# Two chunks share half-height rest products: rest weights split into a high and a low tile, first stage in a fixed order

## The chip, the cores and the metric

The kernel runs on one core of one Trainium2 chip. The metric is device time in microseconds (us) of one execution; lower is better. TensorE (PE) multiplies, with a sequencer that issues weight loads (PEld) and matmuls; VectorE (DVE), ScalarE (ACT) and GpSimd (POOL) work elementwise; SyncE (SP) issues most transfers.

## The reference

A causal depthwise convolution with 7 softmaxed taps per head, followed by two gated feed-forward layers on 8192 tokens (2 sequences of 4096) of 192 features, with 2048 hidden features.

```python
w = softmax(weight)                                  # 8 heads x 7 taps
out[b, s, h] = sum_k w[h, k] * x_pad[b, s + k, h]    # 24 features per head
x = out.reshape(8192, 192)

h = x @ w_in;  g = h * np.clip(h + 3.0, 0.0, 6.0) / 6.0;               y = g @ w_out     # layer 1
h = y @ w_in2; g = np.where(h > 0, h, np.exp(np.minimum(h, 0)) - 1.0); z = g @ w_out2    # layer 2
```

## The kernel before, in words

**Tiles.** Tokens are taken in 16 blocks of 512 (256 of each sequence), on the free axis; features lie on partitions. The hidden features of a layer are 16 chunks of 128. A "chunk" in this text is one (layer, block, chunk) triple; there are 512 of them, in the list `slots` (lines 526 to 533). Block 0 and block 1 of layer 0 are interleaved by twos, then come the other blocks in turn.

**Precision.** The operands of a product are each split into a high part and a low remainder, and a product is the sum high x high, high x low, low x high. 192 features are one full tile of 128 partitions ("main") and a rest of 64. Main of the block is in the tiles opA (high) and opB (low); the rest's high and low parts lie in opC and opD, a part in either half of the partitions. Weights: `h` and `l` for main (128 partitions), and one tile `r` for the rest, in which the high part lies in the lower 64 partitions and the low part in the upper for even chunks, and the other way round for odd chunks.

**First product** (`mm1`, line 461): into one PSUM bank `h` of 128 hidden features x 512 tokens; there are three such banks. At full height (`half` = ALL) it is five matmuls: h x opA, h x opB, l x opA, r x opC, r x opD. At half height the lower and the upper 64 partitions are done by separate matmuls, three and either one or two of the rest for each half: five and four.

**Gate** (`gate`, line 485; `first_done`, line 724): ACT makes u from h (one operation in layer 0, two in layer 1), DVE makes g from u and h, which frees the bank. `split` then makes gh (ACT) and gl (DVE) of the chunk before. `run_jobs` (line 569) spends a budget of other work after each chunk: decoding, splitting and loading of weights (`prepare`, line 654), convolution of later blocks, splitting of the second layer's input, sums; jobs have due chunks, and what is due is issued whatever the budget.

**Second product** (`mm2`, line 506): five matmuls per height from gh, gl and wo into two banks, four chunks after the first product (LAG = 4).

**Order.** The start (line 673) is written out by hand, up to block 0's operands. The first 36 chunks (line 764) run at full height, for each chunk a first product, its gate and jobs, then the second product of the chunk four before; within this stage a scheduler orders the instructions of each engine. From there to the end (line 765) the order is by hand again: two streams, one for the lower 64 partitions and one for the upper, alternate matmul by matmul, the upper one BEHIND = 8 matmuls later. In a bank the upper half may start only when the lower has left it (a tiny POOL memset, `relay`, line 479, passes that on). The convolution's taps of blocks 0 and 1 are tensor products (`taps_tensor`, line 280, 28 matmuls), those of the others run on DVE.

Of the kernel before, what the change touches and what calls it, by code (L numbers as in the profile page):

```python
# [8 lines left out]
F32 = mybir.dt.float32  # L9
# [19 lines left out]
NB = 512  # L29
# [25 lines left out]
def conv_moe_moe2(ctx: ExitStack, tc: tile.TileContext, x, weight, w_in1, w_out1, w_in2, w_out2, out):  # L55
# [95 lines left out]
    def split_w(item, f):  # L151

        kind, l, a, e = item
        if kind == "out":
            v = f[:, :(e - a) * D].rearrange("p (f e) -> p f e", f=e - a)
            w = wo[l][:, a:e]
            act.copy(w[:, :, 0:D], v)
            yield  # L160
            for c0, c1, to in ((0, P, 2 * P), (P, D, D)):
                vec.tensor_tensor(out=w[:, :, to:to + c1 - c0], in0=v[:, :, c0:c1],
                                  in1=w[:, :, c0:c1].bitcast(F32), op=ALU.subtract)
            yield
            return
        w = {k: v[:, a * P:e * P] for k, v in wi[l].items()}
        if kind == "in":
            f = f[:, :(e - a) * P]
            act.copy(w["h"], f)
            yield  # L170
            vec.tensor_tensor(out=w["l"], in0=f, in1=w["h"].bitcast(F32), op=ALU.subtract)
        else:
            f = f[:, :(e - a) // 2 * P].rearrange("p (f c) -> p f c", c=P)
            r = w["r"].rearrange("p (f two c) -> p two f c", two=2, c=P)
            for k, h in enumerate((LO, UP)):
                act.copy(r[h, k], f[h])
            yield
# [120 lines left out]

    def conv_r(b):
        a = yield from taps_vector(b, 1)  # L300
        lh, hl = opnd[0, b][2:]
        T0, T1 = slice(0, HB), slice(HB, NB)
        act.copy(hl[LO, T0], a[LO])
        act.copy(lh[UP, T1], a[UP])
        yield
        act.copy(lh[UP, T0], a[LO])
        act.copy(hl[LO, T1], a[UP])
        yield
        vec.tensor_tensor(out=lh[LO, T0], in0=a[LO], in1=hl[LO, T0].bitcast(F32), op=ALU.subtract)
        vec.tensor_tensor(out=hl[UP, T1], in0=a[UP], in1=lh[UP, T1].bitcast(F32), op=ALU.subtract)  # L310
        yield
        act.copy(hl[UP, T0], lh[LO, T0].bitcast(F32))
        act.copy(lh[LO, T1], hl[UP, T1].bitcast(F32))
        yield

    def conv(b):
        opnd[0, b] = ring()
        yield from alternate(conv_main(b, taps_tensor if b < TENSOR_TAPS else taps_vector), conv_r(b))

    CONV = 2 * K + 6  # L320

    def ring():


        A = op.tile([P, NB], F32R, name="opA", tag="opA")
        Bt = op.tile([P, NB], F32R, name="opB", tag="opB")
        lh = op.tile([P, NB], F32R, name="opC", tag="opC")
        hl = op.tile([P, NB], F32R, name="opD", tag="opD")
        return A, Bt, lh, hl

    def feed(b):
        load_squares(b)
# [106 lines left out]

    def split_y(b):  # L440
        y0, yr = ys.pop(b)
        A, Bt, lh, hl = opnd[1, b] = ring()
        act.copy(A, y0)
        yield
        h, other = (UP, LO) if b % 2 else (LO, UP)
        hi, lo = (lh, hl) if b % 2 else (hl, lh)
        act.copy(hi[h], yr[h])
        vec.tensor_tensor(out=Bt, in0=y0, in1=A.bitcast(F32), op=ALU.subtract)
        yield
        act.copy(lo[other], hi[h].bitcast(F32))  # L450
        vec.tensor_tensor(out=lo[h], in0=yr[h], in1=hi[h].bitcast(F32), op=ALU.subtract)
        yield
        act.copy(hi[other], lo[h].bitcast(F32))
        yield


# [4 lines left out]
    def mm1(s, half):  # L461


        l, b, f = slots[s]
        A, Bt, lh, hl = opnd[l, b]
        w = {k: v[half, f * P:(f + 1) * P] for k, v in wi[l].items()}
        if half is not UP:
            hs[s] = ps_h.tile([P, NB], F32, name="h", tag="h")
        h = hs[s]
        low, high = half is not UP, half is not LO  # L470
        todo = [(w["h"], A), (w["h"], Bt), (w["l"], A)]
        if half is ALL or low == (f % 2 == 0):
            todo += [(w["r"], lh), (w["r"], hl)]
        else:
            todo += [(w["r"], hl if low else lh)]
        for i, (k, m) in enumerate(todo):
            mm = nc.tensor.matmul(h, k, m[half], start=low and i == 0, stop=high and i == len(todo) - 1)  # L477
# [56 lines left out]
    NS = len(slots)  # L534
    at = {sl: i for i, sl in enumerate(slots)}
    jobs = []
    WORK = {"first": 3883, "conv": 8522, "split": 1664, ("sum", 0): 1304, ("sum", 1): 2488}

    def alternate(*gens):
        gens = list(gens)  # L540
# [21 lines left out]
    def load(item):  # L562

        kind, _, a, e = item
        n = (e - a) * {"out": D, "in": P, "r": R}[kind]
        lo = {"out": n + 160, "in": n + 80, "r": 2 * n + 160}[kind]
        return n // 2 + 80 + n + 80 + lo + (2 * n + 180) // 5

    def run_jobs(s):
# [103 lines left out]
    with tc.manual_schedule():  # L673
        tp, tr = load_taps(), transposes(0)
        make_identity(nc, ident)
        load_rows(0)
        next(tp)
        ahead(0)
        nc.gpsimd.memset(three, 3.0)
        next(tp)  # L680
        next(tr)
        next(tr)
        for k in range(K):
            vec.tensor_scalar(out=diag[k], in0=ident, scalar1=taps[:, 0, k:k + 1], scalar2=None, op0=ALU.mult)
        for _ in range(2):
            next(main)
        r = conv_r(0)
        while ready[0] < FIRST0:
            next(weights)
            next(r, None)  # L690
        drain(r)
        load_rows(1)
        drain(main)
# [51 lines left out]
    sums = {}  # L745
    BOTH = at[0, 2, 0]

    def stream(half, slots1, behind):

        for s in slots1:  # L750
            if s < NS:
                yield from mm1(s, half)
            ends = s >= behind and half is UP and slots[s - LAG][2] == NF - 1
            if s < NS and half is not LO and not ends:
                first_done(s)
            if s >= behind:
                yield from mm2(s - LAG, half)
                second_done(s - LAG, half)
            if s < NS and ends:
                first_done(s)  # L760
            if s == NS - 1 and half is not LO:
                split(s)

    drain(stream(ALL, range(BOTH + LAG), LAG))
    with tc.manual_schedule():
        ends = {}
        n = {LO: 0, UP: BEHIND}
        for half in (LO, UP):
            for s in range(BOTH + LAG, NS + LAG):
                first = 5 if (half is LO) == (slots[s % NS][2] % 2 == 0) else 4  # L770
                if s < NS:
                    assert half is LO or n[half] > ends[s]
                    n[half] += first
                    ends[s] = n[half]
                n[half] += 5
        lower, upper = (stream(half, range(BOTH + LAG, NS + LAG), LAG) for half in (LO, UP))
        for _ in range(BEHIND):
            next(lower)
        going = [lower, upper]
        while going:  # L780
            for g in list(going):
                if next(g, jobs) is jobs:
                    going.remove(g)
        run_jobs(NS + 9)


# [28 lines left out]
```

## Time and profile before

| | |
|---|---|
| median of 3 runs | 1174.16 us (1173.98 to 1175.13) |
| the profiled execution | 1174.62 us |
| its span, first to last instruction | 1172.9 us |
| PE / PEld / DVE / ACT busy | 99% / 89% / 78% / 79% |
| stage at full height | about 15.8 to 102.8 us |
| two half-height streams | 102.8 to about 1166.5 us |

A row of the timeline gives the start (us from the span's start), the duration, the engine, the line, the operation, the tiles written and read, shapes and how many instructions were merged, and in brackets the idle time of the engine before it and what ended it. "64*128" is the height and width of a matmul's weights: 64 partitions contracted, 128 columns. A matmul's end is modelled and includes the way through the array, so successive matmuls overlap; the distance of their starts is what a matmul takes. L49 is the line of a helper through which all DVE and ACT operations go.

### The profile page before, as it was taken

How to read it: one execution, taken by the hardware profiler on the slowest of the kernel's cores; microseconds unless marked ns; L12 is line 12 of the kernel's file. 1: busy time of each engine (PE TensorE's matmuls, PEld its weight loads, DVE VectorE, ACT ScalarE, POOL GpSimd, SP SyncE). 2: the span in 40 equal slices, each digit the busy share in tenths (PEclk: the TensorE clock that was granted, in tenths of full speed). 3: DMA queues.
4: the chain of work that ended last, by engine and by line, in shares of the span. 5: the costliest groups of instructions: out<-in, count | busy, mean ns of one | idle time of the engine just before them, and what ended most of it. 6: DMA issues, size and time to landing. Idle time of an engine off the chain costs nothing.

```text
span 1172.9 us, 25129 instructions
## 1 busy us (share of the span) xinstructions
PE 1163.0 (99%) x9504; PEld 1045.5 (89%) x9504; DVE 919.7 (78%) x1560; ACT 929.8 (79%) x1684; POOL 44.9 (4%) x490
## 2 busy tenths in 40 slices
PE   8999999999999999999999999999999999999998
PEld 6778999999998889988899888997889998878777
DVE  7997999988887878868787787877877666677765
ACT  6876777778869787786877869778686888888885
POOL 0000000000000000000000000000000000000000
PEclk9999999999999999999999999999999999999999
DMA  6422011110010100101001010100000000000001
GB/s 181 107 67 42 20 42 46 29 28 1 2 28 1 28 1 5 25 1 28 2 11 18 1 29 1 21 9 1 15 2 15 2 8 8 15 15 15 13 6 26
DMA packets 105370, 26.80 MB, mean 23 GB/s; under 512 B 96416, under 2 KB 104096, under 8 KB 105248
## 3 DMA queue, kind: packets, MB, share of 16 engines
q1 hardware_dynamic: 104960, 24.99, 10.2%
q8 instruction: 74, 1.21, 0.4%
q14 instruction: 48, 0.39, 0.1%
q10 hardware_dynamic: 288, 0.20, 0.1%
HBM read 18.87 MB, written 6.29 MB: 21 GB/s over the span
## 4 chain that ended last, share of the span: by engine, by line
PE 97%; DVE 1%; ACT 1%; issue 0%; ACTq 0%; DVEq 0%
PE p L521 49%; PE h L477 47%; DVE acc L49 0%; ACT u L49 0%; DVE xw L49 0%; DVE wi0r L49 0%; ACT gh L49 0%; ACT opC L49 0%; ACT xw L49 0%; DVE cw L49 0%; PE pso L427 0%; ACT L49 0%; DVE wo L49 0%; ACT opD L49 0%; PE psx L243 0%
## 5 line engine op out<-in xcount | busy, mean ns | idle before, releaser
L521 PE MATMUL p<-gh,wo 64*128 64x512 f32 (+1 forms) x2976 | 639.9, 393 | 0.2 <-ACT gh L49 0.2
L49 DVE SCALAR_TENSOR_TENSOR g<-u,h 128x512 f32<-128x512 f32 x512 | 350.6, 685 | 222.7 <-ACT u L49 219.5
L521 PE MATMUL p<-gl,wo 64*128 64x512 f32 (+1 forms) x1984 | 517.7, 391 | 0.0
L521 PEld LDWEIGHTS p<-gh,wo 64*128 64x128 f32 (+1 forms) x2976 | 461.6, 185 | 34.2 <-ACT gh L49 0.7
L49 DVE TENSOR_TENSOR gl<-g,gh 128x512 fp32r<-128x512 f32 x512 | 350.3, 684 | 2.2 <-ACT gh L49 1.7
L521 PEld LDWEIGHTS p<-gl,wo 64*128 64x128 f32 (+1 forms) x1984 | 313.3, 161 | 17.0 <-DVE gl L49 0.5
L49 ACT CAST gh<-g 128x512 fp32r<-128x512 f32 x512 | 311.1, 608 | 10.4 <-DVE g L49 10.2
L49 ACT ACTIVATE u<-h,three 128x512 f32<-128x512 f32 x256 | 176.1, 688 | 139.1 <-PE h L477 137.6
L477 PE MATMUL h<-opA,wi1h 64*128 64x512 f32 x512 | 200.0, 399 | 0.0
L477 PE MATMUL h<-opA,wi1l 64*128 64x512 f32 x512 | 199.3, 398 | 0.0
L477 PE MATMUL h<-opB,wi1h 64*128 64x512 f32 x512 | 195.7, 390 | 0.0
L49 ACT ACTIVATE u<-h 128x512 f32<-128x512 f32 x256 | 152.6, 596 | 51.8 <-PE h L477 50.6
L477 PE MATMUL h<-opA,wi0h 64*128 64x512 f32 (+1 forms) x476 | 182.1, 396 | 0.5 <-DVE g L49 0.5
L477 PE MATMUL h<-opA,wi0l 64*128 64x512 f32 (+1 forms) x476 | 181.8, 395 | 0.0
L477 PE MATMUL h<-opB,wi0h 64*128 64x512 f32 (+1 forms) x476 | 180.5, 391 | 0.0
L49 ACT ACTIVATE u<-u 128x512 f32<-128x512 f32 x256 | 161.9, 632 | 8.1
L477 PE MATMUL h<-opD,wi1r 64*128 64x512 f32 x384 | 148.7, 393 | 0.0
L477 PE MATMUL h<-opC,wi1r 64*128 64x512 f32 x384 | 147.8, 390 | 0.0
L477 PE MATMUL h<-opD,wi0r 64*128 64x512 f32 (+1 forms) x366 | 141.0, 393 | 0.0
L477 PE MATMUL h<-opC,wi0r 64*128 64x512 f32 (+1 forms) x366 | 140.3, 391 | 0.6 <-ACT opC L49 0.6
L477 PEld LDWEIGHTS h<-opA,wi1h 64*128 64x128 f32 x512 | 94.2, 184 | 14.0 <-DVE g L49 5.2
L49 DVE SCALAR_TENSOR_TENSOR acc<-xT,taps,acc 128x256 f32<-128x256 f32 (+1 forms) x180 | 106.0, 601 | 0.1
(90 smaller groups left out, 1217.8 us busy)
## 6 DMA issues: line engine op xcount, KB each, us to landing
raw<-in_moe_w_out_dram SPq DMA_DIRECT2D x16, 384.0 KB, 3.3
out_dram<-z SPq DMA_DIRECT2D x180, 32.0 KB, 1.6
raw<-in_moe_w_in_dram SPq DMA_DIRECT2D x7, 512.0 KB, 4.5
x_sq<-in_x_dram SPq DMA_DIRECT2D x112, 32.0 KB, 2.2
raw<-in_moe_w_in_dram SPq DMA_DIRECT2D x8, 256.0 KB, 4.0
xr_sq<-in_x_dram SPq DMA_DIRECT2D x56, 32.0 KB, 2.1
x_sb<-in_x_dram SPq DMA_DIRECT2D x4, 128.0 KB, 3.7
raw<-in_moe_w_in_dram SPq DMA_DIRECT2D x4, 128.0 KB, 3.6
```

The costliest lines, as they stand in the source:

```text
L49: return fn(*args, **kw)
L477: mm = nc.tensor.matmul(h, k, m[half], start=low and i == 0, stop=high and i == len(todo) - 1)
L521: nc.tensor.matmul(p[:n], k[:, :n], m[half], start=first and not end and k is not w0l, stop=last and end == 1)
```

## The change

The tile `r` becomes two tiles of half the width, `r` (high) and `s` (low); in each, even chunks lie in the lower 64 partitions and odd chunks in the upper. opC and opD now hold the rest's high and low part in both halves alike. So the three rest products of a chunk (r x opC, r x opD, s x opC) are all half-height ones, for an even chunk in the lower half and for an odd one in the upper.

In the first 36 chunks two chunks are multiplied together (`mm1_pair`): six full-height matmuls, alternately for the one and the other chunk, and then six half-height ones, alternately lower half (even chunk) and upper half (odd chunk), into two banks. Then both gates with their jobs, then the second products of the two chunks four before, at full height as before. In the later stage the half of a chunk that holds its rest does six first-product matmuls, the other half three; the order of the first three is h x opA, l x opA, h x opB; BEHIND is 9.

The whole kernel now is in a fixed order. In the start, block 1's rows are loaded before block 0's taps; its convolution is written out (tensor taps behind the first pair, the rest's taps around the first gates) instead of being a job; weights are prepared up to FIRST = 4 instead of 5 pieces before the first pair. Splitting a piece of rest weights is one copy and one subtraction on 128 partitions instead of two each on 64.

```diff
-BEHIND = 8
+BEHIND = 9
-FIRST0 = 1
-FIRST = 5
-TENSOR_TAPS = 2
+FIRST = 4
...
-    wi = [{n: const.tile([P, FF], F32R, name=f"wi{l}{n}") for n in ("h", "l", "r")} for l in range(2)]
+    wi = [{n: const.tile([P, FF // (1 + (n in "rs"))], F32R, name=f"wi{l}{n}") for n in "hlrs"} for l in range(2)]
...
-            for k, h in enumerate((LO, UP)):
-                act.copy(r[h, k], f[h])
-            yield
-            for k, h, o in ((0, LO, UP), (1, UP, LO)):
-                vec.tensor_tensor(out=r[o, k], in0=f[h], in1=r[h, k].bitcast(F32), op=ALU.subtract)
+        pre = kind == "r"
+        hi, lo = (wi[l][k][:, (a >> pre) * P:(e >> pre) * P] for k in ("rs" if pre else "hl"))
+        f = f[:, :(e - a >> pre) * P]
+        act.copy(hi, f)
+        yield
+        vec.tensor_tensor(out=lo, in0=f, in1=hi.bitcast(F32), op=ALU.subtract)
...
-        todo = [(w["h"], A), (w["h"], Bt), (w["l"], A)]
-        if half is ALL or low == (f % 2 == 0):
-            todo += [(w["r"], lh), (w["r"], hl)]
-        else:
-            todo += [(w["r"], hl if low else lh)]
+        todo = w[0] + w[1] * ((half is LO) == (f % 2 == 0))
...
+    def first_parts(l, b, f, half):
+
+        A, Bt, C, Dt = opnd[l, b]
+        main = slice(f * P, (f + 1) * P)
+        rest = slice(f // 2 * P, (f // 2 + 1) * P)
+        return [(wi[l][k][half, main], m[half]) for k, m in (("h", A), ("l", A), ("h", Bt))], \
+               [(wi[l][k][half, rest], m[half]) for k, m in (("r", C), ("r", Dt), ("s", C))]
+
+    def mm1_pair(s):
+
+        pair = (s, s + 1)
+        parts = []
+        for t, half in zip(pair, (LO, UP)):
+            assert slots[t][2] % 2 == (half is UP)
+            hs[t] = ps_h.tile([P, NB], F32, name="h", tag="h")
+            parts.append(first_parts(*slots[t], ALL)[0] + first_parts(*slots[t], half)[1])
+        for i in range(6):
+            for t, todo in zip(pair, parts):
+                nc.tensor.matmul(hs[t], *todo[i], start=i == 0, stop=i == 5)
...
+    r, tr = conv_r(0), transposes(1)
+    next(main)
+    next(main)
+    for _ in range(K):
+        next(weights)
+        next(r)
+    for g in (r, r, weights, main, r, tr, r, tr, main):
+        next(g)
     while ready[0] < FIRST:
         next(weights)
-    drain(transposes(1))
...
-    job(conv(1), CONV, 0, at[0, 1, 0], WORK["first"])
...
-    drain(stream(ALL, range(BOTH + LAG), LAG))
...
+    opnd[0, 1] = ring()
+    main, r = conv_main(1, taps_tensor), conv_r(1)
+    mm1_pair(0)
+    next(main)
+    next(main)
+    for _ in range(3):
+        next(r)
+    for t in range(2):
+        raw_g[t] = gate(0, hs.pop(t))
+        split(t - 1)
+        next(r)
+        next(r)
+    for g in (r, r, main):
+        next(g)
+    drain(r)
+    drain(main)
+    for s in range(2, BOTH + LAG, 2):
+        mm1_pair(s)
+        for t in (s, s + 1):
+            first_done(t)
+        if s >= LAG:
+            for t in (s, s + 1):
+                drain(second(t - LAG, ALL))
```

## Rows read from the trace of the kernel before

**Rows 1.** The page, busy time: busy us, share of the span, instructions.
```profile
PE 1163.0 (99%) x9504; PEld 1045.5 (89%) x9504; DVE 919.7 (78%) x1560; ACT 929.8 (79%) x1684; POOL 44.9 (4%) x490
```
**Rows 2.** The page, chain that ended last, by engine.
```profile
PE 97%; DVE 1%; ACT 1%; issue 0%; ACTq 0%; DVEq 0%
```
**Rows 3.** The chain of waits in order of time: start, us, engine, tile, matmuls.
```profile
31.38 1.20 PE h L477 x4
...
33.04 1.17 PE h L477 x5
...
101.69 1.16 PE p L521 x5
...
160.59 0.93 PE h L477 x8
```
**Rows 4.** Windows: stretch, its length, busy us of each engine (instructions), clock, DMA.
```profile
31.38:102.69 71.31, 71.31 (x306) 55.96 (x306) 67.12 (x125) 55.79 (x101) 0.00 (x0) 1.00 0.29 74
```
**Rows 5.** Timeline near the end, PE and weight loads after a common standstill.
```profile
1162.57 0.19 PEld L521 LDWEIGHTS p<-gh,wo 64*128 64x128 f32 x2 [0.67 <-ACT gh L49]
1162.58 0.50 PE L521 MATMUL p<-gh,wo 64*128 64x512 f32 x2 [0.24 <-ACT gh L49]
```
**Rows 6.** Timeline where the stage at full height ends.
```profile
102.23 0.63 PE L521 MATMUL p<-gl,wo 128*128 128x512 f32 x2
102.23 0.19 PEld L521 LDWEIGHTS p<-gl,wo 128*128 128x128 f32 x1
...
102.78 0.18 PEld L477 LDWEIGHTS h<-opA,wi0h 64*128 64x128 f32 x1 [0.36 <-issue]
...
103.12 0.39 PE L477 MATMUL h<-opB,wi0h 64*128 64x512 f32 x1
```
**Rows 7.** Timeline in the start: from 8 rows to 128.
```profile
4.31 0.57 PE L207 MATMUL pt<-etap,heads 8*128 8x7 f32 x2
...
4.81 0.18 PEld L243 LDWEIGHTS psx<-ident,x_sb 128*128 128x128 f32 x1
```
**Rows 8.** Timeline of PE in the front: first matmul and waits.
```profile
15.76 0.96 PE L477 MATMUL h<-opA,wi0h 128*128 128x512 f32 x3
16.55 0.43 PE L477 MATMUL h<-opB,wi0h 128*128 128x512 f32 x1
...
27.23 0.50 PE L477 MATMUL h<-opA,wi0h 128*128 128x512 f32 x1 [0.47 <-DVE g L49]
...
31.38 0.50 PE L477 MATMUL h<-opC,wi0r 128*128 128x512 f32 x1 [0.63 <-ACT opC L49]
```
**Rows 9.** Timeline: last matmul of a chunk, its u and its g.
```profile
101.29 0.40 PE L477 MATMUL h<-opD,wi0r 128*128 128x512 f32 x1
...
101.79 0.69 ACT L49 ACTIVATE u<-h,three 128x512 f32<-128x512 f32 x1 [0.26 <-PE h L477]
...
102.51 0.69 DVE L49 SCALAR_TENSOR_TENSOR g<-u,h 128x512 f32<-128x512 f32 x1 [0.26 <-ACT u L49]
```
**Rows 10.** The chain of waits at the end of the kernel.
```profile
1160.58 0.15 PE h L477
...
1162.58 3.96 PE p L521 x22
```
**Rows 11.** Waits of the weight loader from 104.4 to 1162.5: us, times, longest.
```profile
PEld h L477 <- DVE g L49: 5.2, 17, 0.3
```
**Rows 12.** Timeline before the wait at 362.24 (13 waits are like this).
```profile
355.92 0.40 PE L477 MATMUL h<-opD,wi1r 64*128 64x512 f32 x1
...
356.35 0.60 ACT L49 ACTIVATE u<-h 128x512 f32<-128x512 f32 x1 [0.56 <-PE h L477]
...
362.24 0.18 PEld L477 LDWEIGHTS h<-opA,wi1h 64*128 64x128 f32 x1 [0.32 <-DVE g L49]
```
**Rows 13.** Timeline of PE at the wait at 368.87 (4 waits are like this).
```profile
368.87 0.50 PE L477 MATMUL h<-opA,wi1h 64*128 64x512 f32 x1
...
369.91 0.39 PE L477 MATMUL h<-opD,wi1r 64*128 64x512 f32 x1
```

More of the change, by code (lines that the diff above doesn't have):

```diff
@@ L300, in conv_r @@
         a = yield from taps_vector(b, 1)
-        lh, hl = opnd[0, b][2:]
+        C, Dt = opnd[0, b][2:]
         T0, T1 = slice(0, HB), slice(HB, NB)
-        act.copy(hl[LO, T0], a[LO])
-        act.copy(lh[UP, T1], a[UP])
+        act.copy(C[LO, T0], a[LO])
+        act.copy(C[UP, T1], a[UP])
         yield
-        act.copy(lh[UP, T0], a[LO])
-        act.copy(hl[LO, T1], a[UP])
+        act.copy(C[UP, T0], a[LO])
+        act.copy(C[LO, T1], a[UP])
         yield
-        vec.tensor_tensor(out=lh[LO, T0], in0=a[LO], in1=hl[LO, T0].bitcast(F32), op=ALU.subtract)
-        vec.tensor_tensor(out=hl[UP, T1], in0=a[UP], in1=lh[UP, T1].bitcast(F32), op=ALU.subtract)
+        vec.tensor_tensor(out=Dt[LO, T0], in0=a[LO], in1=C[LO, T0].bitcast(F32), op=ALU.subtract)
+        vec.tensor_tensor(out=Dt[UP, T1], in0=a[UP], in1=C[UP, T1].bitcast(F32), op=ALU.subtract)
         yield
-        act.copy(hl[UP, T0], lh[LO, T0].bitcast(F32))
-        act.copy(lh[LO, T1], hl[UP, T1].bitcast(F32))
+        act.copy(Dt[UP, T0], Dt[LO, T0].bitcast(F32))
+        act.copy(Dt[LO, T1], Dt[UP, T1].bitcast(F32))
         yield
@@ L317, in conv @@
         opnd[0, b] = ring()
-        yield from alternate(conv_main(b, taps_tensor if b < TENSOR_TAPS else taps_vector), conv_r(b))
+        yield from alternate(conv_main(b, taps_vector), conv_r(b))
     CONV = 2 * K + 6
[L322 to L329, printed above, removed]
     def feed(b):
@@ L441, in split_y @@
         y0, yr = ys.pop(b)
-        A, Bt, lh, hl = opnd[1, b] = ring()
+        A, Bt, C, Dt = opnd[1, b] = ring()
         act.copy(A, y0)
@@ L445, in split_y @@
         h, other = (UP, LO) if b % 2 else (LO, UP)
-        hi, lo = (lh, hl) if b % 2 else (hl, lh)
-        act.copy(hi[h], yr[h])
+        act.copy(C[h], yr[h])
         vec.tensor_tensor(out=Bt, in0=y0, in1=A.bitcast(F32), op=ALU.subtract)
         yield
-        act.copy(lo[other], hi[h].bitcast(F32))
-        vec.tensor_tensor(out=lo[h], in0=yr[h], in1=hi[h].bitcast(F32), op=ALU.subtract)
+        act.copy(C[other], C[h].bitcast(F32))
+        vec.tensor_tensor(out=Dt[h], in0=yr[h], in1=C[h].bitcast(F32), op=ALU.subtract)
         yield
-        act.copy(hi[other], lo[h].bitcast(F32))
+        act.copy(Dt[other], Dt[h].bitcast(F32))
         yield
@@ L464, in mm1 @@
         l, b, f = slots[s]
-        A, Bt, lh, hl = opnd[l, b]
-        w = {k: v[half, f * P:(f + 1) * P] for k, v in wi[l].items()}
-        if half is not UP:
+        w = first_parts(l, b, f, half)
+        if half is LO:
             hs[s] = ps_h.tile([P, NB], F32, name="h", tag="h")
         h = hs[s]
-        low, high = half is not UP, half is not LO
-        todo = [(w["h"], A), (w["h"], Bt), (w["l"], A)]
-        if half is ALL or low == (f % 2 == 0):
-            todo += [(w["r"], lh), (w["r"], hl)]
-        else:
-            todo += [(w["r"], hl if low else lh)]
+        todo = w[0] + w[1] * ((half is LO) == (f % 2 == 0))
         for i, (k, m) in enumerate(todo):
-            mm = nc.tensor.matmul(h, k, m[half], start=low and i == 0, stop=high and i == len(todo) - 1)
+            mm = nc.tensor.matmul(h, k, m, start=half is LO and i == 0, stop=half is UP and i == len(todo) - 1)
             if half is LO and i == len(todo) - 1:
@@ L536, in conv_moe_moe2 @@
     jobs = []
-    WORK = {"first": 3883, "conv": 8522, "split": 1664, ("sum", 0): 1304, ("sum", 1): 2488}
+    WORK = {"conv": 8522, "split": 1664, ("sum", 0): 1304, ("sum", 1): 2488}
     def alternate(*gens):
@@ L672, in conv_moe_moe2 @@
     main = conv_main(0, taps_tensor)
[L673 to L693, printed above, removed]
+    ctx.enter_context(tc.manual_schedule())
+    tp, tr = load_taps(), transposes(0)
+    make_identity(nc, ident)
+    load_rows(0)
+    next(tp)
+    ahead(0)
+    load_rows(1)
+    nc.gpsimd.memset(three, 3.0)
+    next(tp)
+    next(tr)
+    next(tr)
+    for k in range(K):
+        vec.tensor_scalar(out=diag[k], in0=ident, scalar1=taps[:, 0, k:k + 1], scalar2=None, op0=ALU.mult)
+    r, tr = conv_r(0), transposes(1)
[6 more added lines that the diff above has]
+        next(g)
     while ready[0] < FIRST:
         next(weights)
-    drain(transposes(1))
     job(weights, 0, 0, pace)
-    job(conv(1), CONV, 0, at[0, 1, 0], WORK["first"])
     for b in range(2, NBLK):
@@ L746, in conv_moe_moe2, with second, stream @@
     BOTH = at[0, 2, 0]
-    def stream(half, slots1, behind):
+    def second(s, half):
+        yield from mm2(s, half)
+        second_done(s, half)
+    def stream(half, slots1):
         for s in slots1:
@@ L752, in stream @@
                 yield from mm1(s, half)
-            ends = s >= behind and half is UP and slots[s - LAG][2] == NF - 1
-            if s < NS and half is not LO and not ends:
+            ends = half is UP and slots[s - LAG][2] == NF - 1
+            if s < NS and half is UP and not ends:
                 first_done(s)
-            if s >= behind:
-                yield from mm2(s - LAG, half)
-                second_done(s - LAG, half)
+            yield from second(s - LAG, half)
             if s < NS and ends:
@@ L760, in stream @@
                 first_done(s)
-            if s == NS - 1 and half is not LO:
+            if s == NS - 1 and half is UP:
                 split(s)
-    drain(stream(ALL, range(BOTH + LAG), LAG))
[L765 to L784, printed above, removed]
+    opnd[0, 1] = ring()
@@ new lines, in conv_moe_moe2 @@
+    ends = {}
+    n = {LO: 0, UP: BEHIND}
+    for half in (LO, UP):
+        for s in range(BOTH + LAG, NS + LAG):
+            if s < NS:
+                assert half is LO or n[half] > ends[s]
+                n[half] += 6 if (half is LO) == (slots[s][2] % 2 == 0) else 3
+                ends[s] = n[half]
+            n[half] += 5
+    lower, upper = (stream(half, range(BOTH + LAG, NS + LAG)) for half in (LO, UP))
+    for _ in range(BEHIND):
+        next(lower)
+    going = [lower, upper]
@@ L788 @@
+    while going:
+        for g in list(going):
+            if next(g, jobs) is jobs:
+                going.remove(g)
+    run_jobs(NS + 9)
 _INS = ["x", "weight", "moe_w_in", "moe_w_out", "moe2_w_in", "moe2_w_out"]
```

10 lines of the change are left out of this document (1 added, 9 removed).

## The prediction

> **What bounds the kernel now.** I read the page's busy times first: TensorE (PE) is busy 99% of the span, VectorE (DVE) and ScalarE (ACT) under 80% [rows 1]. The reader should not stop there, so I went to the chain of waits: 97% of the span runs through PE [rows 2]. In order of time, that chain is unbroken from 31.38 us to 102.69 us in groups of five matmuls of 1.16 to 1.17 us, so one full-height matmul takes a slot of 0.233 us; later eight half-height ones take 0.93 us, so two of them, one on each half of the rows, share a slot of 0.233 us [rows 3]. By windows, PE has no free time from 31.38 to 102.69 us; DVE is busy 67.12 us of these 71.31 us [rows 4]. So an edit is worth what it changes in PE's slots or in PE's waits, and DVE is a close second in the first 36 chunks.
>
> The sum is made against the profiled execution (1174.62 us, span 1172.9). The median of the runs is 0.46 us lower; I add the sum to the median for the prediction.
>
> **1. Slots removed.** In the first 36 chunks a chunk's first product is five full-height matmuls, ten for a pair. After: six full-height, then six half-height, which go two to a slot, three slots. Ten slots become nine: 18 pairs x 0.233 = 4.19 us less. That two half-height matmuls start together after a common standstill is seen at 1162.57 us (two weight loads and two matmuls, each pair with one start) [rows 5]; I count no stagger.
>
> **2. Height switches added.** Each pair goes from 128 rows to 64 and back: 36 switches. (The one at the end of the stage exists before and after.) What one costs: at 102.23 us the last two full matmuls start (the second 0.23 later, at 102.46), and the next matmul uses 64 rows. Its weight load starts only at 102.78, after 0.36 us in which the loader waited for nothing the profile shows, whereas the load at 102.23 began beside a running matmul. The second half-height matmul starts at 103.12 [rows 6]. From 102.46 to 103.12 are 0.66 us where two slots are 0.47: a switch down costs 0.19 us. The way back isn't in the trace in this shape. Nearest row: at 4.81 us a 128-row weight load follows matmuls on 8 rows, and it too starts just before the last of them ends (4.31 + 0.57 = 4.88; there 102.46 + 0.39 = 102.85 against 102.78, both 0.07 us before that end) [rows 6, 7]. So bounds for the way back are 0 (if the load can be pulled ahead) and 0.19; I take 0.19, as the same 0.07 us tells of the same emptying of the array. 36 x 0.19 = 6.98 us (0.194 unrounded).
>
> The Trainium skill, "TensorEngine Tiling (Array Packing)", Tiling Modes, says that a change of the tiling mode, not of the tile alone, drains TensorE. The row agrees for the way down; by that rule the way back drains too, and the two items come to +2.8 us; by the one row alone they would be -0.7 us.
>
> Items 1 and 2 together: +2.8 us. The removed slot (0.233) is smaller than a switch there and back (0.39).
>
> **3. Front.** The first matmul of a chunk starts at 15.76 us, after the tensor taps of block 0, which don't change. From there to 102.69 are 86.9 us, for 340 full matmuls (79.2 us) and 28 tap matmuls (6.0 us): 1.7 us are lost in waits, the visible ones before 16.55 (the low part of the operand), 27.23 (g of an earlier chunk) and 31.38 (a rest operand of block 1) [rows 8]. In the fixed order the pair multiplies four times by the high operand before it needs the low one (4 x 0.233 = 0.93 us against a subtraction of 0.7), so the first wait goes; block 1's rest operands are made while PE does 28 tap matmuls, so the third goes. But two pairs then follow each other with no second product between, and only three banks exist: the fourth chunk after a gate still open has to wait for g. From the last matmul of a chunk to u 0.50 us, to g 0.72 more, g 0.69 [rows 9]: 1.9 us, of which a switch and a slot (0.43 + 0.23) hide 0.6 to 0.7, so about 1.3 us is late next, and some 0.2 for weights due at the sixth chunk, which DVE makes later. So -0.2 us; bounds -1.7 (no wait left) and +1.4 (one more such wait).
>
> **4. Later pairs.** From the third pair on ten second-product slots (2.33 us) stand behind each pair, and its g must be there for the next pair's second chunk: 1.96 us by the same rows, slack some 0.8 us where before five matmul groups (5.8 us) lay between. DVE, 94% busy, gets the longer period (10 + 9 slots and two switches, 4.8 us), which helps; but an ACT copy that waits for a DVE job now holds up the next u. Mostly hidden: +0.3 us; bounds 0 and 16 pairs x 0.3 = 4.8. The halved weight splitting (one copy and one subtraction for two) lies beside PE: nothing. Loads of block 1's rows issued earlier on the SP queue: nothing, as DVE idles before block 0's low operand.
>
> **5. Steady stage.** Nine first-product slots a pair and ten second-product slots on each half, before and after: 5 and 4 become 6 and 3. BEHIND 9 makes the upper half end one slot later, and the end hangs on its last first product (1160.58, then u, gh and from 1162.58 the second products) [rows 10]: +0.23 us. An odd chunk's upper part now ends one slot later in the pattern too. PE stands still for g 17 times, 5.2 us of loader idle [rows 11]. Thirteen are like 362.24: the chain behind it starts at an odd chunk's end (355.92, u at 356.35) [rows 12] and holds a chunk whose lower part starts one slot later now as well (four-matmul odd chunk, 29 to 30): unchanged. Four are like 368.87, where the held chunk has five matmuls (an even one) and its place doesn't move [rows 13]: the same late chain costs a slot more, 4 x 0.23 = +0.9 us. Bounds 0 (ACT's queue takes it up) and 17 x 0.23 = 3.9.
>
> Sum: -4.2 + 7.0 - 0.2 + 0.3 + 0.2 + 0.9 = +4.0 us: 1178.6 for an execution like the profiled one, 1178.2 from the median.
>
> **Rivals.**
> A, faster: half-height loads are pulled ahead across a switch, because the 0.36 us at 102.78 belong to that place (a stage border) and not to the switch. Place: 36 switches; price 7.0 us back: 1174.2 - 4.2 + 1.2 (items 3 to 5) = 1171.2. It beats the present kernel where a switch costs under (4.2 - 1.2) / 36 = 0.08 us. For it: two halves do run in one slot [rows 3, 5]. Against: the loader's idle time has no releaser, and the 8-row case looks the same [rows 6, 7]. The Trainium skill, "TensorEngine Tiling (Array Packing)", Overview, allows up to twofold speed for contractions of at most 64 rows; the shared slot agrees, and that rule alone gives this rival's 1171.2.
> B, no change: only the way down costs. 18 x 0.19 - 4.2 + 1.2 = +0.4: 1174.6. For it: the way back has no row in this shape.
> C, much slower: the gates of the pair loop become the bound. If each of 16 pairs waits 0.25 us for g (ACT's queue behind DVE), +4 on top: 1182.2. For it: DVE at 94% [rows 4]; against: the longer period leaves it about a tenth free.
>
> **How the numbers follow.** Chances: forecast 0.56, A 0.14, B 0.12, C 0.18. 0.2% is 2.3 us, about what can be told from no change here: faster is under 1171.8, slower over 1176.5. A spreads over that lower edge by item 3's bounds (0.08 faster, 0.06 same); B is mostly same (0.09, the rest on either side); the forecast's lower bounds (item 3 at -1.7, item 5 at 0) reach 1175.6, which gives same 0.09; C is slower. With a little for a front better than I can see: faster 0.14, same 0.24, slower 0.62. Range: from A's 1171.0 to C's 1182.0; outside it some 0.15. The forecast's own range is 1175.6 to 1181.
>
> **What would show it.** Step 1: in a pair, two h matmuls of 64 rows with one start, three times. Step 2: before the first 64-row and the first following 128-row weight load an idle time of the loader named "issue" of some 0.3 us, and 0.43 us from matmul start to matmul start instead of 0.23; a pair with its second products 4.8 us, not 4.43. Step 3: a wait for g of over 1 us at the third pair. Step 5: 17 waits for g, four of them longer. The prediction is wrong if the pair's period is under 4.66 us (then A or B), or over 5.1 (C).

## The result, and the profile after

The changed kernel takes 1184.85 us (median of 5 runs, 1184.12 to 1185.36) against 1174.40 us of the kernel before in the same runs: 1.0088 times as long, 95% interval [1.0073, 1.0103], so 10.4 us slower. The prediction was 1178.2 us, range 1171 to 1182. The sign was right, the size was not (+10.4 us against +4.0), and the time is outside the range.

The page after, busy times and the chain's shares by engine (answering to [rows 1, 2]):

```profile
PE 1169.1 (99%) x9540; PEld 985.3 (83%) x9540; DVE 916.4 (77%) x1555; ACT 924.6 (78%) x1679; POOL 44.8 (4%) x490
...
PE 93%; ACT 4%; DVE 2%; issue 0%; DMA 0%; DVEq 0%
```

TensorE is still 99% busy, but of the chain 4% now run through ACT and 2% through DVE, where both had 1%. Where that lies is seen in the chain of waits after, in order of time (start, us, what; to be read against [rows 3, 10]):

```profile
26.64 0.40 ACT opC L47
27.07 0.40 ACT opC L47
27.49 0.40 ACT opC L47
27.91 0.10 ACT opC L47
...
28.22 0.57 ACT opA L47
...
28.82 0.40 ACT opD L47
29.25 0.41 ACT opD L47
...
29.68 0.70 ACT u L47
...
30.40 0.70 DVE g L47
...
31.14 4.08 PE h L477 x11
35.22 3.44 PE p L515 x10
...
106.01 2.29 PE h L477 x12
108.29 2.52 PE p L515 x10
...
1170.32 0.14 PE h L451
...
1172.30 4.20 PE p L515 x23
```

Three things can be read there. From 26.6 to 31.1 us the chain does not run through TensorE at all, where [rows 3, 8] had only short waits. Right behind it ten second products take 3.44 us, while the same ten take 2.52 us at 108.29 us. And at the end the lone second products start at 1172.30 and take 4.20 us, against 3.96 in [rows 10].

The span grew by 10.2 us (1172.9 to 1183.1). Cut at the start of the first product, at the first weight load of the stage of halves and at the last lone second products, it divides so:

| stretch | before, us | after, us | difference |
|---|---|---|---|
| start to the first product (15.76; 15.33) | 15.76 | 15.33 | -0.4 |
| front: first product to the halves (102.78; 110.74) | 87.0 | 95.4 | +8.4 |
| steady stage, to 1162.58; 1172.30 | 1059.8 | 1061.6 | +1.8 |
| from there to the end of the span | 10.3 | 10.8 | +0.5 |

The last half microsecond is the 0.24 us by which the last second products take longer, and about as much behind them.

The timeline of one pair's end, TensorE and its weight loads after (answering to [rows 6]):

```profile
106.78 0.63 PE L477 MATMUL h<-opB,wi0h 128*128 128x512 f32 x2
...
107.33 0.19 PEld L477 LDWEIGHTS h<-opC,wi0r 64*128 64x128 f32 x2 [0.36 <-issue]
107.33 0.50 PE L477 MATMUL h<-opC,wi0r 64*128 64x512 f32 x2
...
107.67 0.39 PE L477 MATMUL h<-opD,wi0r 64*128 64x512 f32 x2
107.90 0.40 PE L477 MATMUL h<-opC,wi0s 64*128 64x512 f32 x2
...
108.22 0.53 PEld L515 LDWEIGHTS p<-gh,wo 128*128 128x128 f32 x3 [0.36 <-issue]
...
109.02 0.62 PE L515 MATMUL p<-gl,wo 128*128 128x512 f32 x2
```

Two half-height matmuls share one start, three times (107.33, 107.67, 107.90). The loader stands still 0.36 us, released by nothing that the profile shows, before the first half-height load and before the first full-height one. The way back can now be priced: from the last two half-height matmuls at 107.90 to the matmul at 109.02 are 1.12 us for four slots, which without a switch take 0.93 us; that is 0.19 us, as on the way down. And the pair that starts at 106.01 takes 2.29 + 2.52 = 4.81 us.

Windows of the kernels before and after over the front (stretch, length, then busy us of PE, PEld, DVE, ACT, POOL with instructions, granted clock, DMA share, GB/s). Before:

```profile
12.00:18.00 6.00, 5.98 (x31) 4.85 (x30) 5.06 (x14) 5.90 (x15) 0.00 (x0) 1.00 0.67 182
12.00:40.00 28.00, 26.88 (x120) 21.28 (x119) 26.07 (x56) 24.82 (x53) 0.00 (x0) 1.00 0.62 154
```

After:

```profile
12.00:18.00 6.00, 5.98 (x32) 4.42 (x31) 2.16 (x6) 4.57 (x13) 0.00 (x0) 1.00 0.17 56
26.00:32.00 6.00, 1.78 (x7) 0.96 (x4) 3.71 (x8) 4.09 (x9) 0.00 (x0) 0.86 0.01 3
32.00:36.00 4.00, 4.00 (x12) 2.31 (x12) 3.19 (x8) 2.03 (x5) 0.00 (x0) 0.50 0.21 58
32.00:40.00 8.00, 8.00 (x28) 5.07 (x27) 6.88 (x17) 6.03 (x12) 0.00 (x0) 0.68 0.48 123
12.00:40.00 28.00, 23.76 (x101) 17.09 (x99) 19.19 (x43) 19.00 (x42) 0.00 (x0) 0.88 0.34 95
```

DVE is busy 19.19 of the 28 us, where it was 26.07: in the fixed order it stands still for almost 7 us more, and it does 43 instructions instead of 56. TensorE's 8 busy us from 32 to 40 hold only 28 matmuls, at a granted clock of 0.68 in the mean (0.50 from 32 to 36 us).

### The profile page after: what moved, and what is told of

The parts are those of the page before. It is cut to its first block, busy times and chain, and to the rows that moved or that the text cites. A ratio compares the mean times of both kernels' runs of the same rounds, so it can differ in the third digit from the quotient of the medians.

```text
span 1183.1 us, 25204 instructions
## 1 busy us (share of the span) xinstructions
PE 1169.1 (99%) x9540; PEld 985.3 (83%) x9540; DVE 916.4 (77%) x1555; ACT 924.6 (78%) x1679; POOL 44.8 (4%) x490
## 4 chain that ended last, share of the span: by engine, by line
PE 93%; ACT 4%; DVE 2%; issue 0%; DMA 0%; DVEq 0%
PE p L515 47%; PE h L451 42%; PE h L477 3%; ACT u L47 2%; ACT opC L47 1%; PE psc L276 1%; DVE g L47 1%; ACT gh L47 1%; DVE acc L47 0%; DVE gl L47 0%; ACT yr L47 0%; DMA traw<-in_weight_dram 0%; PE psx L233 0%; PE pso L408 0%; ACT opD L47 0%
## 5 line engine op out<-in xcount | busy, mean ns | idle before, releaser
L515 PE MATMUL p<-gh,wo 64*128 64x512 f32 (+1 forms) x2976 | 660.2, 394 | 0.5 <-ACT gh L47 0.5
L515 PE MATMUL p<-gl,wo 64*128 64x512 f32 (+1 forms) x1984 | 535.6, 391 | 0.0
L451 PE MATMUL h<-opB,wi1h 64*128 64x512 f32 x512 | 203.1, 399 | 0.0
L451 PE MATMUL h<-opA,wi0h 64*128 64x512 f32 x440 | 171.7, 396 | 0.0
L451 PE MATMUL h<-opB,wi0h 64*128 64x512 f32 x440 | 171.2, 395 | 0.0
L451 PE MATMUL h<-opA,wi0l 64*128 64x512 f32 x440 | 169.4, 390 | 0.0
L451 PEld LDWEIGHTS h<-opA,wi1h 64*128 64x128 f32 x512 | 94.2, 184 | 19.2 <-DVE g L47 7.4
L451 PEld LDWEIGHTS h<-opA,wi1l 64*128 64x128 f32 x512 | 94.7, 185 | 9.3
L451 PEld LDWEIGHTS h<-opB,wi1h 64*128 64x128 f32 x512 | 94.6, 185 | 8.8
L451 PE MATMUL h<-opD,wi1r 64*128 64x512 f32 x256 | 100.5, 394 | 0.0
L451 PE MATMUL h<-opC,wi1s 64*128 64x512 f32 x256 | 99.5, 390 | 0.0
```

Source lines behind the costliest of these rows:

```text
L451: mm = nc.tensor.matmul(h, k, m, start=half is LO and i == 0, stop=half is UP and i == len(todo) - 1)
L515: nc.tensor.matmul(p[:n], k[:, :n], m[half], start=first and not end and k is not w0l, stop=last and end == 1)
```

## The experiments

Times are medians; the kernel before gave 1174.2 to 1174.3 us in all shared runs, the changed kernel is 1184.85. "Front" is, as above, from the first product to the first load of the halves. Each edit is to the changed kernel, unless it says otherwise.

**Switches.** e3_switch issues one half-height pair of products first, so that each pair has four switches.

```
-        for i in range(6):
+        order = (3, 0, 1, 2, 4, 5)
+        for i in order:
...
```

> In each of the 18 pairs one of the three half-height steps comes first and the other two last, so that a pair has four switches of height instead of two, with the same matmuls. Theory (a switch costs 0.19 us in either direction): 36 more switches, a pair's period of 5.20 us for 4.81, and 7 us more: about 1191.8. Rival (it is the step down alone that costs): 18 x 0.19 = 3.5 us more, 1188.3. Rival (the switch is hidden, the period has another cause): 1184.9.

Measured: 1191.37 us, +6.5. Its chain shows one pair's first and second products:

```profile
101.86 2.69 PE h L478 x10
104.55 2.53 PE p L516 x10
107.08 2.68 PE h L478 x11
```

5.22 us a pair against 4.81: two switches more cost 0.41 us. So 0.2 us a switch holds in another order too, and the rival by which only the step down costs (5.00 us a pair) is out.

**The fixed order undone, or alone.** e5_sched takes the kernel before, with its planner and its start, and gives it the changed layout, products, pairs and BEHIND 9:

```
-    drain(stream(ALL, range(BOTH + LAG), LAG))
+    for s in range(0, BOTH + LAG, 2):
+        mm1_pair(s)
...
```

> The start and the scheduled first stage of the kernel before, with the pairs, the weight tiles and the streams of the changed kernel; only the fixed order is undone. Theory (switches 2.7 us, streams 2.0, the fixed order of the start the other 5.7): pairs of 4.81 us, streams of 1066.6 us, no long standstill and no fall of the clock, about 1179.1. Rival (the pair loop with three banks brings the standstills in any order): at least 4 us of standstill between 24 and 40 us again, 1183 or more.

Measured: 1180.37 us. Front 90.2 us; by the window below DVE is as busy as before the change, the clock stays at 1.00.

```profile
12.00:40.00 28.00, 26.65 (x117) 18.26 (x115) 26.05 (x56) 24.07 (x52) 0.00 (x0) 1.00 0.66 170
```

From 16 us to the halves TensorE has one wait in e5, where the changed kernel has two of 2.43 and 1.79 us:

```profile
29.76 0.50 PE L488 MATMUL h<-opA,wi0h 128*128 128x512 f32 x1 [0.28 <-DVE g L49]
```

As e5 keeps the pairs and the three banks, neither of them makes the standstills by itself. The changed kernel takes 4.5 us of its 10.4 more than e5; "fixed order" stands here for all that e5 undoes, the start, the convolution of block 1 written out and the order of every engine in the first stage. e4_full keeps the fixed order and has the products and the layout of before (ten full-height products a pair, no switch, BEHIND 8).

> The changed kernel's order in the start and in the first 36 chunks, with the products, weight tiles and streams of the kernel before: five full-height matmuls a chunk, 5 and 4 in the streams, 8 matmuls behind. Theory: without the switches the pairs save 2.7 us, the streams 2.0 us, and the front's loss stays, so about 1180.2, with the clock still falling after 31 us. Rival (the half-height steps cause the front's standstills too): the front loss goes as well, about 1174.5.

Measured: 1181.93 us, 1.7 us above what was expected. The front is 94.6 us: 7.5 us over the kernel before without a switch in its pairs. The steady stage is as long as before. The quicker TensorE only reaches late operands sooner: the chain of waits runs through ACT and DVE until 49.47 us, where that of the changed kernel is back on TensorE at 31.14, and two more waits for g stand in it, of 1.26 us at 39.09 and of 0.78 us at 49.47.

```profile
48.12 0.58 ACT u L47
48.73 0.70 DVE g L47
49.47 2.36 PE h L466 x9
```

So the two costs don't add up. The switches alone (e5) lengthen the front by 3.2 us, the fixed order alone (e4) by 7.5 us, both together by 8.4 us.

**What holds TensorE up in the front.** e1_front issues block 1's rest taps ahead of the weights of later chunks; e15_gate_first also puts the second pair and its gates ahead of them; e10_early only moves three steps of the weights ahead of the first operands, where DVE stands idle; e11_early_rest is e1 with e10's edit, e16_gate_early is e15 with it.

```
 # e1
-    while ready[0] < FIRST:
-        next(weights)
...
+    next(r)
+    for _ in range(3):
+        next(weights)
+        next(r)
     mm1_pair(0)
...
     drain(main)
 # e15, e16: the second pair and its gates stand here
+    while ready[0] < FIRST:
+        next(weights)
 # e10, e11, e16
-    for g in (r, r, weights, main, r, tr, r, tr, main):
+    for g in (r, r, *[weights] * 4, main, r, tr, r, tr, main):
```

> Block 1's rest taps and copies go ahead of the later weights, and its first high copy ahead of nothing else that waits. Theory (the front's order costs some 5.7 us: two standstills of PE between 26 and 31 us, and the clock that they bring down): both standstills shrink to about 1.3 us in all, the granted clock stays at its upper level, and the time falls by 4 to 6 us against the changed kernel, to about 1179.5. Rival (the pair loop itself, two pairs with no second product between and three banks, makes the standstills): the standstill before the second chunk of the third pair stays above 2 us, the clock falls as before, and the time stays within 1.5 us of 1184.9.

> The changed kernel, with three more steps of the weight preparation issued before the first product's operands (into the 2.26 us before 15.31 us in which DVE stands still, and ACT 1.28 us). Theory (the fixed order leaves DVE and ACT idle early, and TensorE pays for it from 26 us on): some 2 us of DVE's idle time are filled, so the rest taps and u(2) come about 1.5 to 2 us earlier, the standstills at 26.02 and 28.84 us shrink by as much, and fewer matmuls run at the lower clock: 1182.0 (span 1180.3). Rival (DVE's idle time in the front is slack, and the front is bound by the ping-pong behind 18 us alone): within 0.7 us of the changed kernel, 1184.8.

> As the run with the rest taps issued before the later weights, and with the three weight steps before the first operands too. Theory (the weights that must be ready by the sixth chunk hold DVE and ACT, in whatever order): the weights that stood ahead of the third chunk's u are now done before 15.3 us, u(2) comes some 2 us earlier, the standstill of 3.96 us falls to about 2, no matmul runs at the lower clock: 1180.5. Rival (u is held by its own place in ACT's queue, not by the amount of work ahead of it): as the run with the rest taps alone, 1183.4.

> As the run with the rest taps first (1183.4), and the second pair with its u and gh now stands ahead of the later weights in ACT's and DVE's program. Theory (u(2) and g(2) are late because of what stands ahead of them on ACT, four to five copies at 28.9 us in that run, and the bank that they free is what the sixth chunk waits for): u(2) at 26.4 to 27, the sixth chunk starts at 27.8 to 28.5 instead of 30.35, no matmul at the lower clock; front 94.2 to 91.5, time 1180.7. Rival (the weights for the seventh and eighth chunk, now later, take it back at the next pair): front within 0.7 us of 94.2, 1183.2.

> As the run before, with three steps of the weights ahead of the first operands too (they fill DVE's idle time before 15.3 us). Theory (order and idle time together are the whole loss of the front, so both edits give back nearly what undoing the fixed order did): front 91 or less, 1180.0. Rival: front 93 to 94, 1182.8.

Measured, with DVE's busy time in the window 12 to 40 us (a step of the weights is one stretch of their decoding or splitting):

| kernel | DVE busy, us | front, us | time, us |
|---|---|---|---|
| after | 19.19 | 95.4 | 1184.85 |
| e15_gate_first | 19.69 | 95.2 | 1184.33 |
| e1_front | 19.59 | 94.2 | 1183.36 |
| e11_early_rest | 20.61 | 94.1 | 1183.09 |
| e10_early | 20.30 | 93.4 | 1182.80 |
| e16_gate_early | 22.14 | 91.7 | 1181.24 |
| e5_sched | 26.05 | 90.2 | 1180.37 |

e1, e11 and e15 went against my theory: each took the wait away that it was aimed at, and a later chunk waited instead. e1 even shows what its rival foretold, a wait of 3.46 us before the second chunk of the third pair; it is e5, with a wait of 0.28 us, that speaks against the three banks as the cause. TensorE's waits in e15_gate_first (timeline, idle time and its releaser in brackets):

```profile
28.54 0.50 PE L477 MATMUL h<-opA,wi0h 128*128 128x512 f32 x1 [1.13 <-DVE g L47]
37.51 0.50 PE L477 MATMUL h<-opA,wi0h 128*128 128x512 f32 x1 [3.67 <-DVE g L47]
```

and in e16_gate_early:

```profile
28.09 0.50 PE L477 MATMUL h<-opA,wi0h 128*128 128x512 f32 x1 [1.13 <-DVE g L47]
35.01 0.50 PE L477 MATMUL h<-opA,wi0h 128*128 128x512 f32 x1 [1.85 <-DVE g L47]
```

The first wait is the same, 1.13 us; the second is half as long when three steps of the weights were already done in DVE's idle time. The better order alone gives 0.5 us, and e15's runs overlap those of the changed kernel; the filled idle time alone gives 2.0, both together 3.6. So the order is worth some 1.6 us, but only behind the filled idle time. The front goes with the work that DVE has done by then, though not run by run in the table (e11 has more done than e10 and a longer front), and DVE's busy time is also a result, as gates wait for TensorE; e10 and e13 are the tests that change it from outside.

e13_light tests this from the other side: it leaves out DVE's two decode instructions of the first ten pieces of weights. e14_before_light does the same to the kernel before, as a control.

```
+        if ready[0] >= LIGHT:
             vec.tensor_scalar(out=c[:, :n], ...
...
+        if ready[0] >= LIGHT:
             vec.scalar_tensor_tensor(out=xi[:, :n], ...
```

> The changed kernel without the two DVE instructions (cw and xw, together 0.7 to 1.1 us) that decode each of the first ten pieces of weights: their values are left wrong, everything else is issued in the same order. Theory (in the fixed order it is the back and forth of DVE and ACT over the weights that holds up block 1's rest taps and u(2), and with them TensorE from 26 us on): about 2.2 us of DVE steps stand before the rest taps' end, so the standstills at 26.02 and 28.84 shrink by 2 to 3 us in sum, the lower clock with them: front 95.4 to 91.5, time 1181. Rival (the order of copies and gates alone, opC before opA and u(2), holds TensorE up, and DVE's load doesn't matter): front within 0.7 us of 95.4, 1184.5.

> The control: the kernel before without the same two DVE instructions for its first ten pieces of weights. Its front (87.0 us) loses only 1.65 us in waits, so both theories expect little: between 1172.8 and 1174.2.

Measured: 1182.05 us, front 92.9, and 1175.15 us for the control. With the same order and less DVE work 2.8 us come back, which the control doesn't show: it is 0.9 us longer, above what was expected, though not clear of no change (ratio 1.0007 [0.9998, 1.0016]). The stretch from opA over u to g (28.84 to 31.14 in the changed kernel) stays at 2.3 us with less for DVE to do; behind opA's copy two copies of opD stand ahead of u in ACT's program. The front lies between the two theories, nearer to the first.

**The lower clock.** e2_warm has 19 extra fp32 matmuls of 256 columns into a free bank while TensorE stands still; e2b_warm_short, whose edit is shown, has 9.

```
+                if s == 4 and i == 0:
+                    warm(5 if t == s else 4)
...
```

> 19 matmuls whose result is read by nobody are added where PE stands still ahead of and inside the third pair; nothing else changes. Theory (the matmuls from 31 to 37 us take 0.43 us each because PE stood still before): the granted clock stays at its upper level from 16 to 48 us, those matmuls take 0.233 us, and the time falls by 2 to 2.7 us to about 1182.4. Rival (they are slow for another reason, as waits for operands): the clock falls as before and the time stays at 1184.9 or rises.

> As the kernel with 19 added matmuls, but 5 and 4 of them, since each took 0.43 us and not 0.22 and the 19 outlasted the standstill by 3.8 us; these take 2.2 and 1.7 us. Theory (the low clock after the standstill costs 2.7 us by itself): no slow matmuls, the second chunk of the third pair still starts at about 31.1 us, and 2.2 to 2.7 us less than the changed kernel: about 1182.4. Rival (what PE gains, the DVE and ACT chain behind the weights takes back, as a chain that holds the front until some 40 us): under 1 us less.

Measured: 1185.96 and 1184.99 us. In both no matmul runs slower, the window 12 to 40 us has the clock at 1.00. But in e2b TensorE then waits at the next pair:

```profile
38.30 0.50 PE L479 MATMUL h<-opA,wi0h 128*128 128x512 f32 x1 [2.02 <-DVE g L47]
```

The 2.9 us that the slow matmuls seem to cost (7.5 us from 31.14 to 38.65, where a pair without its first matmul takes 4.6) are not there to be won: at full clock TensorE reaches the next late gate sooner and waits there. e2's 19 matmuls outlasted the standstill.

**The steady stage.** e6_mirror is the changed kernel with even and odd chunks exchanged between the halves (six and three turned, BEHIND 6), e8_before_mirror the kernel before in the same way (BEHIND 7).

```
-        todo = w[0] + w[1] * ((half is LO) == (f % 2 == 0))
+        todo = w[0] + w[1] * ((half is UP) == (f % 2 == 0))
...
```

> The changed kernel with the parity of the rest weights turned round (even chunks in the upper half, odd in the lower), so that the streams do 3 and 6 instead of 6 and 3, and the upper stream can run 6 matmuls behind instead of 9 with the same distance in each bank. Theory (the streams' 2.0 us are one matmul at the end, 0.23, and longer and more waits of even chunks for an odd chunk's g, 1.8): three matmuls less at the end (0.7 us), an odd chunk's upper part ends three slots earlier, so the waits of the second kind vanish (10 of 24) and those of the first stay; streams of 1064.0 us instead of 1066.6, about 1182.3. Rival (the waits come from ACT's queue alone, whatever the place of the odd chunk): only the 0.7 us.

> The kernel before, with the parity of its rest tile turned round (4 and 5 instead of 5 and 4) and the upper stream 7 matmuls behind instead of 8; nothing of the change. Theory: one matmul less at the end (0.23 us) and the four waits of even chunks gone (4 x 0.23 to 0.26), 1.2 us less than before: about 1173.1. Rival (these waits don't hang on the parity): 1174.0.

Measured: 1183.27 and 1173.80 us (ratio to before 0.9996 [0.9986, 1.0005]). The weight loader's waits for g in the stage of halves (us, times, longest) after, answering to [rows 11]:

```profile
PEld h L451 <- DVE g L47: 7.6, 23, 0.5
```

and in e6_mirror:

```profile
PEld h L451 <- DVE g L47: 5.1, 15, 0.7
```

17 waits of 5.2 us became 23 of 7.6. The 13 of [rows 12] are still there at 0.31 to 0.34 us each. The four of [rows 13], of 0.27 us, are four of 0.49 to 0.52 us now, a slot longer, as at 377.32:

```profile
377.32 0.18 PEld L451 LDWEIGHTS h<-opA,wi1h 64*128 64x128 f32 x1 [0.52 <-DVE g L47]
```

And six new ones of 0.24 to 0.27 us stand where the kernel before had no wait, as at 448.50. For four of the six (448.50, 591.01, 733.54, 876.06) the load at the same place of the kernel before (439.84, 582.03, 724.23, 866.43) started 0.05 us after its g had ended: one slot later, such a g makes a wait. The two others, at 195.11 and 301.46, stay open.

```profile
448.50 0.18 PEld L451 LDWEIGHTS h<-opA,wi1h 64*128 64x128 f32 x1 [0.24 <-DVE g L47]
```

With the parity turned 15 are left in e6, and from the first load of the halves to the last sum's first product it takes 1.3 us less (1065.3 against 1066.6); waits for y grew there from 0.2 to 1.3 us. In e8 the four of [rows 13] are gone and 13 waits are left, as expected; its time can't be told from no change.

**A version that beats both?** e12_hold_only is the kernel before with one edit in its planner, e9_hold has it on e8_before_mirror: within one position a convolution job takes no step past its last rest tap.

```
+            held[0] = part == 1 and k == K - 1
...
+            held[0] = False
             step(max(going, key=lambda j: j[7]))
+            if held[0]:
+                break
```

> The kernel before, with one edit in its scheduler: within one position a block's convolution job takes no further step after the last of its rest taps, so that ACT isn't given a copy that waits for a DVE instruction issued just before it (ACT opD waits 0.72 us for DVE acc at 359.36, and 13 waits of TensorE for g of about 0.3 us stand behind such places). Theory: most of these 13 go, 13 x 0.27 = 3.5 us less: 1170.8. Rival 1 (what ACT copies later collides elsewhere): within 1 us of before, 1174.3. Rival 2 (the waits come from the late end of an odd chunk alone, as my step 5 has it): 1174.3 and 17 waits as before.

> The kernel before with the parity of the halves turned (which alone gave 1173.8) and with the same edit of the scheduler. Theory: the two gains add, 1170.3. Rival: as the turned kernel alone, 1173.8.

Measured: 1173.27 us (ratio 0.9992 [0.9983, 1.0001]) and 1173.20 us (0.9991 [0.9982, 1.0000]). In e12 the waits for g fell from 17 to 7 and from 5.2 to 2.7 us, but the kernel gains only 1.0 us, at the edge of what can be told from nothing; in e9 the two gains didn't add up either:

```profile
PEld h L480 <- DVE g L49: 2.7, 7, 0.6
PEld h L480 <- ACT opC L49: 0.6, 1, 0.6
```

The twelve waits between 362 and 860 us are all gone, 3.7 us of the loader's idle time, so they did stand behind the copies that the edit holds back; the five from 979 us on stay. But three new waits came near 200 us, two for g (0.50 and 0.58 us) and one for opC (0.58 us). That the gain is smaller still, 1.0 us, stays open.

## Why the prediction was right or wrong

**Steps 1 and 2, slots against switches: right.** The pair's period was to be 4.8 us and is 4.81; 20 slots of the kernel before are 4.66, so 18 pairs cost +2.7 us where +2.8 was predicted. The way back, which no row of before showed in this shape, costs as much as the way down, 0.19 us. The way down shows as two gaps of 0.32 and 0.34 us from start to start in place of 0.233, ahead of 107.33 and of 107.67, and not as the one of 0.43 us that the prediction named as its sign. With that rivals A and B are out. The Trainium skill, "TensorEngine Tiling (Array Packing)", Tiling Modes, says that a change of mode drains TensorE; the measured 0.2 us a switch, both ways, agree.

**Step 3, the front: wrong, and with it the size.** This is the step that failed. It was put at -0.2 us, bounds -1.7 and +1.4, and costs +5.7 us (8.4 less the 2.7 of the switches), +5.3 with the earlier start. The step said that the third wait goes, as "block 1's rest operands are made while PE does 28 tap matmuls". They are not: these matmuls end at 24.1 us, and the last rest tap on DVE ends at 26.6. I had counted instructions for TensorE and dependences, not the order in which ACT and DVE get theirs. These rows of the trace after show what I passed over, DVE's instructions in the start and ACT's behind the taps:

```profile
15.31 0.69 DVE L47 TENSOR_TENSOR opB<-psc,opA 128x512 fp32r<-128x512 f32 x1 [2.26 <-ACT opA L47]
...
17.69 0.43 DVE L47 TENSOR_TENSOR wi0l<-xw,wi0h 128x256 fp32r<-128x256 f32 x1 [1.41 <-ACT wi0h L47]
...
21.97 1.01 DVE L47 SCALAR_TENSOR_TENSOR acc<-xT,taps,acc 128x256 f32<-128x256 f32 x2 [1.22 <-ACT acc L47]
...
26.64 1.67 ACT L47 CAST opC<-acc 64x256 fp32r<-64x256 f32 x4 [2.41 <-DVE acc L47]
28.22 0.57 ACT L47 CAST opA<-psc 128x512 fp32r<-128x512 f32 x1
28.82 0.83 ACT L47 CAST opD<-opD 64x256 fp32r<-64x256 f32 x2
29.68 0.69 ACT L47 ACTIVATE u<-h,three 128x512 f32<-128x512 f32 x1
```

DVE waits for ACT for 4.9 us in three places before 22 us, with other work ready that its fixed program has later: the first time ACT's copy itself waits for the tap matmuls, and three steps of the weights could have been done in that time (e10). Then ACT stands still for 2.41 us in front of a copy that needs DVE's last tap, with opA's copy (its input ready at 24.1) and u of the third chunk (ready at 26.4) queued behind. The step's wait of 1.3 us for g is there, but as the second of two, and at 1.79 us; the first, 2.43 us for block 1's opA, isn't in the step at all. [Rows 4] showed DVE 94% busy in the front: that was the sign that an order which lets it stand still is paid for. I had used it for rival C alone, in the later pairs, where it doesn't bite. That the order of DVE and ACT is the cause is shown in the main: undoing it (e5), filling DVE's idle time (e10) and taking work off DVE (e13) each give time back. Which instruction of the order costs how much is not shown.

**Step 4, later pairs: +0.3 predicted, none found.** From 38.65 us on each pair takes 4.81 us, so rival C's wait per pair is out, though the time came out beyond it. In e4, whose pairs are shorter without switches, such waits do come up to 49 us. The signs of being wrong that the prediction named, a period under 4.66 or over 5.1 us, watched the pairs; none watched the order of the front.

**Step 5, the steady stage: right in kind, too small.** +1.1 us predicted, +2.0 measured. The end is 0.24 us longer, as put (0.23). The late chain was to make four waits longer by one slot, and it did, from 0.27 to 0.5 us. What the step left out are the places where g came just in time before: four of them now wait too, for 1.0 us of the 2.4 us more of the loader's idle time, and two further waits bring 0.5 us. e4, with the old layout, has the old length, and e5, with the new, the new one.

By terms: -4.2 + 7.0 was measured as +2.7, step 3 as +5.3 instead of -0.2, step 4 as 0 instead of 0.3, and step 5 as +2.0 instead of +1.1: 10.0 of the 10.4 us. The split between the switches and step 3 depends on which is taken away first: without the fixed order the switches cost the front 3.2 us (e5), within it 0.8 us (95.4 against 94.6 in e4).

## What to carry to other kernels

When a planned order gives way to one written by hand, read the order of each engine's program, not only the dependences: here an early wait on the second busiest engine was paid for 10 us later on the busiest. A single wait that was moved away came back at a later chunk; compare the busy time of the engine behind in the same window before you believe in the fix. And two half-height products in a slot pay only if the slots saved between two switches exceed their price: here one slot of 0.233 us was saved against 0.4. When an edit makes a chain a slot later, look also at the places where its result came in time by less than a slot.

## What the runs showed of the hardware

TensorE's granted clock was 1.00 in all of the front before. After, it was 0.50 from 32 to 36 us, with full-height matmuls 0.43 us apart instead of 0.233, as these in the timeline:

```profile
31.73 1.05 PE L477 MATMUL h<-opA,wi0l 128*128 128x512 f32 x2
32.59 1.05 PE L477 MATMUL h<-opB,wi0h 128*128 128x512 f32 x2
```

That is the lower of its two levels, 1.2 GHz. Ahead of it TensorE had done one matmul between 26.4 and 31.1 us. In e16_gate_early, which stood still for 1.13 us before 28.09 and for 1.85 us before 35.01, the clock stayed at 1.00 and no matmul was slower.

The cost of a switch was the same, 0.19 to 0.2 us, whichever height came first, and in e3 also where a second product stood ahead of the half-height matmuls.
